# Four units of convolution in one stretch instead of two, on one Trainium2 core

## The chip, the core and the metric

The kernel runs on one core of one Trainium2 chip. A core has five engines with a queue of instructions each: TensorE (PE in the profile, with its weight loads shown apart as PEld), VectorE (DVE), ScalarE (ACT), GpSimd (POOL) and SyncE (SP), and 16 DMA engines that move data between HBM and the on-chip memory. PE writes into PSUM, a small memory of accumulators that DVE and ACT read. The metric is the time of one execution on the device in microseconds (us); lower is better. Engines run their own instructions in order and wait for each other by semaphores.

## What is computed

Two layers, one after the other, on x of shape 8 x 4160 x 192 (batch, sequence, channels). First a causal convolution over 7 positions, whose weights are a softmax and are shared by the 24 channels of each of 8 heads; then a channel mix, in which each position is blended with the one before it:

```python
x_pad = concat([zeros(B, 6, D), x], axis=1)
y     = einsum('hk,bskhg->bshg', softmax(weight), windows(x_pad, 7))   # B=8, S=4160, D=192
prev  = y shifted by one position
xk    = mu_k * y + (1 - mu_k) * prev
xr    = mu_r * y + (1 - mu_r) * prev
k     = relu(xk @ w_k)                    # 192 -> 1024
v     = (k * k) @ w_v                     # 1024 -> 192
out   = sigmoid(xr @ w_r) * v             # float32
```

## The kernel before

**Tiles.** Two batch rows form a pair, and four pairs are worked through one after the other. Channels come in thirds of 64 (`NC` = 3), so that 64 partitions hold one batch row of the pair and 64 the other. The sequence of a pair is cut in *steps* of 512 positions (a few of 256, and one short step at the end that collects the tails).

**Slots and bundles.** A step of 512 has eight *slots*; a slot is one tile of k: six matmuls (`k_mm`), a relu on ACT out of PSUM (`k_relu`), and a square on DVE (`k_square`). Four slots are a *bundle*, and the main loop runs over 65 bundles and a short end; two bundles make a step. Each bundle also has one *quad* of the last stage: `r` (12 matmuls) and its sigmoid `r_out` on ACT, `v_rows` in two halves of 32 matmuls, and `v_out`, a DVE product that reads v from PSUM and after which SP issues two writes to HBM. DVE also blends: `diff`, three `scale` and one `add_y` each for xk and xr, per step.

**Convolution.** It is done on PE as a product with a banded matrix (`toe`), in *units* `(g, c)`: a group `g` of four blocks of 120 positions (three in some groups), and a third `c`. `conv_t` issues eight matmuls a block, of up to 32 columns and 32 rows each, 32 matmuls for a unit of four blocks, and each matmul has its own weight load: 64 PE instructions a unit. `to_yT` then copies the unit from PSUM to `yT`, on ACT or on DVE. In the tables, units from group 3 on are dealt out two to a bundle, from bundle 1 to bundle 50, and `conv_pair` runs them. The first groups are done in the functions of the first bundles.

**The order of the work** is written out by hand (`bundle_rest` for bundle 3 and later). On PE a bundle is: two `k_mm`, a third, `r`, `v_rows` half 0, the fourth `k_mm`, the convolution's units in one stretch, `v_rows` half 1. Here the four `k_mm` are called k0 to k3, the halves v0 and v1. On DVE it is: the last square of the bundle before, a part of the blending, `v_out` of the quad before, more blending and three squares, and, in odd bundles, the copy of the second unit.

**PSUM.** One ring of four places of two banks serves all: each `k_mm`, `r`, `v` and each two units of convolution take one place, which comes free when what reads it is done. Where two engines read the same tile, the recorder lets the second wait for the first: a unit's copy on DVE waits for the copy on ACT of the other unit in that place.

**Loads.** x comes by DMAs that POOL issues (`load_x`, two or four for a group), into eight buffers (`xb`). They are put at the head of a bundle (table `early`), five bundles ahead of the group's first unit, and a tiny DVE memset in `x_tile` keeps them from starting before DVE has come so far. Groups 5 and 6 are loaded in bundle 1 (table `mix_a`), 7 in bundle 2.

**Instructions.** With every loop unrolled, PE's program has 19,957 instructions. A bundle with two units of four blocks has 328 of them: k0 to k2 36, `r` 24, v0 64, k3 12, convolution 128, v1 64. A bundle without convolution has 200.

Of the kernel before, what the change touches and what calls it, by code (L numbers as in the profile page):

```python
# [7 lines left out]
FP32 = mybir.dt.float32  # L8
# [6 lines left out]
def kernel(  # L15
# [11 lines left out]
    nc = tc.nc  # L27
# [5 lines left out]
    P = 128  # L33
# [5 lines left out]
    BANK = 512  # L39
# [13 lines left out]
    ring = ctx.enter_context(tc.tile_pool(name="ring", bufs=4, space=bass.MemoryType.PSUM))  # L53
# [21 lines left out]
    n = 0  # L75
# [9 lines left out]
    groups = []  # L85
# [66 lines left out]
    n = groups[0][2] * 2 * D  # L152
# [120 lines left out]
    def conv_t(g, c, o, blocks):  # L273

        for n, i in enumerate(blocks):
            for first_piece in (True, False):
                for s in range(2):
                    for q in range(2):
                        c0 = c * Q + q * 32
                        lo, hi = c0 // G, (c0 + 31) // G  # L280
                        h, m = (hi, 32) if first_piece else (lo, hi * G - c0)
                        p0 = s * Q + q * 32
                        nc.tensor.matmul(  # L283
                            out=o[p0 : p0 + m, n * BLK : (n + 1) * BLK],
                            lhsT=xbs[g][:, i, s, c0 : c0 + m],
                            rhs=toe[:, h, 0:BLK],
                            start=True,
                            stop=True,
                        )

    def to_yT(g, c, o, copy):
        p, base, nb = groups[g]
        n = min(nb * BLK, S - base)
        copy(out=yTs[p][:, c, YC + base : YC + base + n], in_=o[:, 0:n])  # L294

    def conv_pair(b):

        units = xt.get(b, [])
        if not units:
            return  # L300
        o = ring.tile([P, 2, BANK], FP32, tag="k", name="ps_t")
        for k, (g, c) in enumerate(units):
            if groups[g][1] == 0 and c == 0:
                new_yT(groups[g][0])
            conv_t(g, c, o[:, k, :], range(groups[g][2]))
        for k, (g, c) in enumerate(units):
            to_yT(g, c, o[:, k, :], nc.vector.tensor_copy if k and b % 2 else nc.scalar.copy)

    def new_yT(p):
        yTs[p] = two.tile([P, 3, -(-(YC + S) // 16) * 16], BF16, tag="yT", name="yT")  # L310
        nc.vector.memset(yTs[p][:, :, 0:YC], 0.0)
# [63 lines left out]
    def k_mm(n, cs=range(NC)):  # L375


        s, j = slots[n]
        L = steps[s][2]
        xk = xks[s]  # L380
        if cs[0] == 0 and n not in k_ps:
            k_ps[n] = ring.tile([P, 2, BANK], FP32, tag="k", name="ps_k")
        ps = k_ps[n]
        nf = STEP // L

        for c in cs:
            for f in range(nf):
                fs = slice((j * nf + f) * P, (j * nf + f + 1) * P)
                for i in range(2):
                    r = slice(i * Q, (i + 1) * Q)  # L390
                    nc.tensor.matmul(  # L391
                        out=ps[:, i, f * L : (f + 1) * L],
                        lhsT=wk[r, c, fs],
                        rhs=xk[r, c, :L],
                        start=c == 0 and f == 0,
                        stop=c == NC - 1 and f == nf - 1,
                    )

    def k_relu(n):
        ps = k_ps.pop(n)  # L400
        k_sb = four.tile([P, 2 * STEP], BF16, tag="k_sb", name="k_sb")
        k_sbs[n] = k_sb
        nc.scalar.activation(out=k_sb, in_=ps.rearrange("p a b -> p (a b)"), func=AF.Relu)  # L403

    def k_square(n):
        s, j = slots[n]
        L = steps[s][2]
        k_sb = k_sbs.pop(n)
        if j == 0:
            k2s[s] = three.tile([P, NF, 2 * STEP], BF16, tag="k2", name="k2")  # L410
        nf = STEP // L
        i = k_sb
        o = k2s[s][:, j, :]
        if nf > 1:
            i = k_sb.rearrange("p (b f t) -> p f b t", b=2, f=nf)
            o = k2s[s][:, j * nf : (j + 1) * nf, 0 : 2 * L].rearrange("p f (b t) -> p f b t", b=2)
        nc.vector.tensor_tensor(out=o, in0=i, in1=i, op=ALU.mult)  # L417
# [113 lines left out]
    early, rq, rs, xt, mix_a, mix_b, mix_c, vq, late = ({} for _ in range(9))  # L531

    def at(table, b, fn, *a):
        table.setdefault(b, []).append((fn, a))

    units = [(g, c) for g in range(3, len(groups)) for c in range(NC)]
    for n, u in enumerate(units):
        xt.setdefault(1 + n // 2, []).append(u)
    for g in range(5, len(groups)):
        b = max(1, 1 + (units.index((g, 0))) // 2 - 5)  # L540
        at(mix_a if b == 1 else early, b, x_tile, g)
        at(mix_a if b == 1 else early, b, load_x, g)
    for s, (p, t0, L, n0, ns) in enumerate(steps):
        fb = first_bundle[s]
        if s == 0:
# [26 lines left out]
    for s, j, vb in quads:  # L572
        b = vb - (s == LAST)
# [7 lines left out]
    def run(table, b, part=slice(None)):  # L581
        for fn, a in table.get(b, [])[part]:
            fn(*a)
# [86 lines left out]
    def bundle_second(b, ns):  # L670

        act_, dve_ = nc.scalar.copy, nc.vector.tensor_copy
        g = 2
        k_mm(ns[0])
        k_relu(ns[0])
        k_mm(ns[1])
        tiles = [ring.tile([P, 2, BANK], FP32, tag="k", name="ps_t") for _ in range(2)]
        outs = [tiles[0][:, 0, :], tiles[1][:, 0, :], tiles[0][:, 1, :]]
        conv_t(g, 0, outs[0], range(4))
        to_yT(g, 0, outs[0], dve_)  # L680
        k_relu(ns[1])
        conv_t(g, 1, outs[1], range(4))
        to_yT(g, 1, outs[1], dve_)
        k_mm(ns[2])
        k_relu(ns[2])
        conv_t(g, 2, outs[2], range(4))
        to_yT(g, 2, outs[2], act_)
        k_mm(ns[3])
        k_square(ns[0])
        run(mix_a, b)  # L690
        k_relu(ns[3])
        k_square(ns[1])
        run(mix_b, b)
        conv_pair(b)
        run(mix_c, b)
        run(late, b)

    def bundle_rest(b, ns):

        units = xt.get(b, [])  # L700
        quad = vq[b][0]
        if b == 3:
            for n in range(2):
                k_mm(ns[n])
                k_relu(ns[n])
            k_square(bundles[b - 1][2])
            k_square(bundles[b - 1][3])
            run(mix_a, b)
        else:
            if b == 4:  # L710
                v_out(*vq[b - 1][0])
            k_square(bundles[b - 1][3])
            run(mix_a, b)
            if b > 4:
                v_out(*vq[b - 1][0])
            for n in range(2):
                k_mm(ns[n])
                k_relu(ns[n])
        run(mix_b, b)
        k_square(ns[0])  # L720
        k_square(ns[1])
        run(mix_c, b)
        k_mm(ns[2])
        k_relu(ns[2])
        run(rq, b, slice(0, 1))
        if units:
            run(rs, b, slice(0, 1))
        v_rows(*quad, 0)
        if not units:
            run(rs, b, slice(0, 1))  # L730
        k_square(ns[2])
        k_mm(ns[3])
        k_relu(ns[3])
        run(rq, b, slice(1, None))
        run(rs, b, slice(1, None))
        conv_pair(b)
        v_rows(*quad, 1)
        run(late, b)

    def bundle_third(b, ns):  # L740

        quad = vq[b][0]
        for n in bundles[b - 1][2:]:
            k_square(n)
        run(mix_a, b)
        k_mm(ns[0])
        k_relu(ns[0])
        k_square(ns[0])
        k_mm(ns[1])
        k_relu(ns[1])  # L750
        run(rq, b)
        run(rs, b)
        v_rows(*quad, 0)
        conv_pair(b)
        k_square(ns[1])
        run(mix_b, b)
        run(mix_c, b)
        run(late, b)
        k_mm(ns[2])
        k_relu(ns[2])  # L760
        v_rows(*quad, 1, (0,))
        k_mm(ns[3])
        k_relu(ns[3])
        v_rows(*quad, 1, (1,))
        v_out(*quad)
# [56 lines left out]
```

## Time and profile before

| | |
|---|---|
| median of 3 runs | 449.6 us (448.69 to 449.67) |
| the profiled execution | 451.12 us, of which its span 449.4 us |
| PE busy | 436.4 us of the span |
| DVE, ACT, POOL busy | 388.4, 339.8, 71.5 us |
| granted PE clock | 0.999 of full speed |
| one bundle with two units, steady | 6.79 us (stretches of convolution start at 180.53, 187.31 and 194.10) |
| DMA traffic | 42.22 MB, 94 GB/s on average |

The profile is that of one execution. "Idle before" a group of instructions is time in which its engine had nothing running, with what ended the wait; "issue" there means that nothing which the profile shows held the engine back. PEld is the same engine as PE: weight loads run beside matmuls.

### The profile page before, as it was taken

The page shows a single profiled execution, that of the slowest core. Times are in us where ns is not written, and L with a number is a line of the kernel's source. Part 1 is how long each engine was busy: PE and PEld are TensorE (multiplying, and loading weights), DVE is VectorE, ACT ScalarE, POOL GpSimd, SP SyncE. Part 2 cuts the span into 40 slices and gives each one's busy share as a digit, 9 for nine tenths or more (in the row PEclk, how much of TensorE's full clock was granted, in tenths as well). Part 3 has the DMA queues.
Part 4 walks back from the last instruction along what each step waited for, and adds up shares of the span by engine and source line. Part 5 has one row for each costly group of instructions (what it writes and reads, how often), then busy time and mean ns, then how long its engine had stood idle before and what let it go on. Part 6 is the DMA issues. An engine that isn't in the chain of part 4 may idle for free.

```text
span 449.4 us, 21973 instructions
## 1 busy us (share of the span) xinstructions
PE 436.4 (97%) x9968; PEld 332.3 (74%) x9969; DVE 388.4 (86%) x712; ACT 339.8 (76%) x413; POOL 71.5 (16%) x111
## 2 busy tenths in 40 slices
PE   8689999999999999999999999999999999999996
PEld 5457777777777777777777777777777777777786
DVE  5879898988889888889888898888898899999983
ACT  6768778778678777787787787787787788887771
POOL 8422301111221202012211102122000000000000
PEclk9999999999999999999999999999999999999999
DMA  9995548454545546394555556383321122222223
GB/s 151 173 102 107 88 90 143 82 101 87 97 98 103 87 94 92 91 142 71 106 95 93 97 109 95 88 116 79 82 72 54 59 73 71 73 71 73 73 71 109
DMA packets 74782, 42.22 MB, mean 94 GB/s; under 512 B 39884, under 2 KB 74688, under 8 KB 74688
## 3 DMA queue, kind: packets, MB, share of 16 engines
q0 software_dynamic: 38448, 14.66, 29.9%
q1 hardware_dynamic: 35440, 25.59, 18.1%
q8 instruction: 78, 1.28, 1.2%
q10 hardware_dynamic: 800, 0.57, 0.4%
q14 instruction: 16, 0.13, 0.1%
HBM read 29.89 MB, written 25.56 MB: 123 GB/s over the span
## 4 chain that ended last, share of the span: by engine, by line
PE 94%; issue 2%; DMA 2%; POOL 1%; ACT 0%; DVE 0%; POOLq 0%; DVEq 0%
PE ps_v L479 38%; PE ps_k L391 37%; PE ps_t L283 11%; PE ps_r L448 7%; DMA wk<-in_moe_w_k_dram 2%; PE ps_v L431 1%; POOL wk L195 0%; POOL xb L123 0%; ACT k_sb L403 0%; DVE k L417 0%; ACT yT L294 0%; POOL tap L229 0%; DVE o_sb L515 0%; POOL band L257 0%; POOL band L254 0%
## 5 line engine op out<-in xcount | busy, mean ns | idle before, releaser
L403 ACT ACTIVATE k_sb<-ps_k 128x1024 bf16<-128x1024 f32 x260 | 252.3, 1024 | 86.9 <-PE ps_k L391 82.7
L391 PE MATMUL ps_k<-xk,wk 64*128 64x512 bf16 (+1 forms) x1632 | 191.3, 367 | 1.0 <-DMA wk<-in_moe_w_k_dram 0.7
L479 PE MATMUL ps_v<-wv,k 64*128 64x192 bf16 x4032 | 188.5, 243 | 0.7 <-DVE k L417 0.7
L417 DVE TENSOR_TENSOR k<-k_sb 128x1024 bf16<-128x1024 bf16 x260 | 173.8, 687 | 15.9 <-ACT k_sb L403 15.8
L479 PEld LDWEIGHTS <-k 64*128 64x128 bf16 x4032 | 166.2, 94 | 9.1 <-issue 0.9
L391 PEld LDWEIGHTS <-wk 64*128 64x128 bf16 x1632 | 80.7, 94 | 58.5 <-DMA wk<-in_moe_w_k_dram 1.1
L123 POOL DMA_DIRECT2D xb<-in_x_dram x70 | 52.4, 752 | 239.9 <-PE ps_v L479 83.9
L495 DVE TENSOR_TENSOR o_sb<-ps_v,r_sb 128x768 f32<-128x768 f32 x64 | 60.9, 952 | 8.4 <-PE ps_v L479 5.6
L283 PEld LDWEIGHTS <-xb 128*32 128x32 bf16 (+3 forms) x3360 | 45.7, 94 | 28.4 <-issue 27.6
L283 PE MATMUL ps_t<-toe,xb 128*32 128x120 bf16 (+3 forms) x3360 | 56.3, 219 | 5.5 <-issue 5.1
L459 ACT ACTIVATE r_sb<-ps_r 128x768 bf16<-128x768 f32 x65 | 53.6, 826 | 5.4 <-PE ps_v L479 4.7
L294 ACT CAST yT<-ps_t 128x480 bf16<-128x480 f32 (+3 forms) x81 | 41.5, 544 | 6.3 <-PE ps_t L283 5.8
L448 PEld LDWEIGHTS <-xr 64*128 64x128 bf16 x780 | 35.8, 94 | 13.3 <-issue 0.6
L448 PE MATMUL ps_r<-wr,xr 64*128 64x192 bf16 x780 | 43.0, 243 | 0.0
L294 DVE CAST yT<-ps_t 128x480 bf16<-128x480 f32 (+2 forms) x27 | 17.3, 643 | 26.3 <-ACT yT L294 25.3
L365 DVE TENSOR_SCALAR xr<-d,mu 128x512 bf16<-128x512 bf16 (+1 forms) x102 | 36.9, 366 | 0.0
L365 DVE TENSOR_SCALAR xk<-d,mu 128x512 bf16<-128x512 bf16 (+1 forms) x99 | 32.3, 358 | 0.1
L334 DVE TENSOR_TENSOR d<-yT 128x1536 bf16<-128x1536 bf16 (+4 forms) x36 | 31.1, 865 | 1.5 <-ACT yT L294 1.4
L371 DVE TENSOR_TENSOR xr<-xr,yT 128x1536 bf16<-128x1536 bf16 (+1 forms) x33 | 31.1, 942 | 1.1
L371 DVE TENSOR_TENSOR xk<-xk,yT 128x1536 bf16<-128x1536 bf16 (+3 forms) x33 | 30.3, 919 | 0.1
L318 POOL COPY y_tail<-yT 128x195 bf16<-128x195 bf16 x4 | 1.9, 477 | 44.0 <-ACT yT L294 43.9
L431 PE MATMUL ps_v<-wv,k 128*128 128x192 bf16 x64 | 5.5, 247 | 0.0
(50 smaller groups left out, 44.9 us busy)
## 6 DMA issues: line engine op xcount, KB each, us to landing
out_dram<-o_sb SPq DMA_DIRECT2D x128, 192.0 KB, 3.5
xb<-in_x_dram POOLq DMA_DIRECT2D x56, 192.0 KB, 4.6
xb<-in_x_dram POOLq DMA_DIRECT2D x8, 144.0 KB, 4.2
wk<-in_moe_w_k_dram POOLq DMA_DIRECT2D x4, 192.0 KB, 6.1
xb<-in_x_dram POOLq DMA_DIRECT2D x6, 96.0 KB, 3.2
wv<-in_moe_w_v_dram POOLq DMA_DIRECT2D x1, 384.0 KB, 8.5
xb<-in_x_dram POOLq DMA_DIRECT2D x6, 45.8 KB, 3.1
xb<-in_x_dram POOLq DMA_DIRECT2D x8, 32.2 KB, 3.7
```

The source lines that it names most:

```text
L123: nc.gpsimd.dma_start(out=xb[:, lo:hi, s, :], in_=bass.AP(tensor=x.tensor, offset=x.offset + (b * S + t0 + lo * BLK) * D, ap=[[D, P], [BLK ...
L283: nc.tensor.matmul(out=o[p0 : p0 + m, n * BLK : (n + 1) * BLK], lhsT=xbs[g][:, i, s, c0 : c0 + m], rhs=toe[:, h, 0:BLK], start=True, stop= ...
L294: copy(out=yTs[p][:, c, YC + base : YC + base + n], in_=o[:, 0:n])
L365: nc.vector.tensor_scalar(out=t[:, c, :L], in0=diffs[s][:, c, :L], scalar1=mu[:, i, c : c + 1], scalar2=None, op0=ALU.mult)
L371: nc.vector.tensor_tensor(out=o, in0=o, in1=y_of(s, sl, 0), op=ALU.add)
L391: nc.tensor.matmul(out=ps[:, i, f * L : (f + 1) * L], lhsT=wk[r, c, fs], rhs=xk[r, c, :L], start=c == 0 and f == 0, stop=c == NC - 1 and f ...
L403: nc.scalar.activation(out=k_sb, in_=ps.rearrange("p a b -> p (a b)"), func=AF.Relu)
L417: nc.vector.tensor_tensor(out=o, in0=i, in1=i, op=ALU.mult)
L448: nc.tensor.matmul(out=ps[:, i, k * D : (k + 1) * D], lhsT=xr[q, c, ts], rhs=wr[q, c, :], start=c == 0, stop=c == NC - 1,)
L459: nc.scalar.activation(out=r_sbs[s, j], in_=r_ps.pop((s, j))[:, :, 0 : 2 * D], func=AF.Sigmoid)
L479: nc.tensor.matmul(out=v_ps[s, j][:, bank, k * D : (k + 1) * D], lhsT=k2s[s][q, f, t * P : (t + 1) * P], rhs=wv[q, f, :], start=half == 0 ...
L495: nc.vector.tensor_tensor(out=o_sb.rearrange("p (b t) d -> p b (t d)", b=2), in0=v_ps.pop((s, j)), in1=r_sbs.pop((s, j)), op=ALU.mult,)
```

## The change

Units from the eleventh on are dealt out four at a time, to bundles 6, 8, 10 and so on up to 48 (bundle 50 keeps the single unit that is left, and the odd bundles from 7 on have none). `conv_units` takes one place of the ring for each two units, runs all units of the bundle in one stretch on PE, and then copies them; in a bundle of four, units 0 and 2 are copied by ACT, 1 and 3 by DVE; in a bundle of two, both by ACT. The loads of x are put five bundles ahead of the bundle that now has the group's first unit, but not before bundle 2, always at its head: groups 5 and 6 move from bundle 1 to bundle 2.

```diff
-    def conv_pair(b):
+    def conv_units(b):
 
         units = xt.get(b, [])
-        if not units:
-            return
-        o = ring.tile([P, 2, BANK], FP32, tag="k", name="ps_t")
+        outs = []
         for k, (g, c) in enumerate(units):
             if groups[g][1] == 0 and c == 0:
                 new_yT(groups[g][0])
-            conv_t(g, c, o[:, k, :], range(groups[g][2]))
+            if k % 2 == 0:
+                tile_ = ring.tile([P, 2, BANK], FP32, tag="k", name="ps_t")
+            outs.append(tile_[:, k % 2, :])
+            conv_t(g, c, outs[k], range(groups[g][2]))
         for k, (g, c) in enumerate(units):
-            to_yT(g, c, o[:, k, :], nc.vector.tensor_copy if k and b % 2 else nc.scalar.copy)
+            to_yT(g, c, outs[k], nc.vector.tensor_copy if k % 2 and len(units) > 2 else nc.scalar.copy)
...
     for n, u in enumerate(units):
-        xt.setdefault(1 + n // 2, []).append(u)
+        xt.setdefault(1 + n // 2 if n < 10 else 6 + (n - 10) // 4 * 2, []).append(u)
     for g in range(5, len(groups)):
-        b = max(1, 1 + (units.index((g, 0))) // 2 - 5)
-        at(mix_a if b == 1 else early, b, x_tile, g)
-        at(mix_a if b == 1 else early, b, load_x, g)
+        b = max(2, min(k for k in xt if (g, 0) in xt[k]) - 5)
+        at(early, b, x_tile, g)
+        at(early, b, load_x, g)
```

In the three functions that write out a bundle, the call of `conv_pair(b)` becomes `conv_units(b)`, in the same place.

More of the change, by code (lines that the diff above doesn't have):

```diff
@@ L693, in bundle_second @@
         run(mix_b, b)
-        conv_pair(b)
+        conv_units(b)
         run(mix_c, b)
@@ L735, in bundle_rest @@
         run(rs, b, slice(1, None))
-        conv_pair(b)
+        conv_units(b)
         v_rows(*quad, 1)
@@ L753, in bundle_third @@
         v_rows(*quad, 0)
-        conv_pair(b)
+        conv_units(b)
         k_square(ns[1])
```

## The prediction, made before the changed kernel ran

> **What bounds the kernel now.** I read the shares of the page, then the chain of waits, then PE's timeline at three places, since the change acts on PE's queue.
>
> ```profile
> PE 436.4 (97%) x9968; PEld 332.3 (74%) x9969; DVE 388.4 (86%) x712; ACT 339.8 (76%) x413; POOL 71.5 (16%) x111
> q8 instruction: 78, 1.28, 1.2%
> PE 94%; issue 2%; DMA 2%; POOL 1%; ACT 0%; DVE 0%; POOLq 0%; DVEq 0%
> ```
>
> PE is busy for 97% of the span, and 94% of the chain that ended last is PE; DVE at 86% and ACT at 76% release in time. So the time falls only by what leaves PE's queue or its gaps, and rises by any new gap. The q8 line matters below: 78 packets in 1.28 MB are 16.4 KB each, and 19,957 PE instructions over 78 are 256, so PE's program arrives in pages of 256 instructions.
>
> The price of a stretch is read at the end of the convolution, where it thins out (start, length of the group, engine, line):
>
> ```profile
> 344.34 1.49 PE L479 MATMUL ps_v<-wv,k 64*128 64x192 bf16 x32
> ...
> 350.17 0.81 PE L283 MATMUL ps_t<-toe,xb 128*32 128x120 bf16 x48
> 350.92 1.50 PE L479 MATMUL ps_v<-wv,k 64*128 64x192 bf16 x32
> ...
> 356.75 0.50 PE L283 MATMUL ps_t<-toe,xb 128*32 128x120 bf16 x24
> 357.18 1.50 PE L479 MATMUL ps_v<-wv,k 64*128 64x192 bf16 x32
> ...
> 362.91 1.48 PE L479 MATMUL ps_v<-wv,k 64*128 64x192 bf16 x32
> ```
>
> From one v1 to the next is 6.58 us with 48 matmuls of convolution, 6.26 with 24, 5.73 with none; with 64 a bundle takes 6.79. From 24 to 64 that is 0.53 us for 40 matmuls, 13.25 ns each (6.6 ns per instruction). Drawn back to none it leaves 6.79 - 64 x 0.01325 - 5.73 = 0.21 us that a stretch costs whatever its length.
>
> The gaps are read at the start:
>
> ```profile
> 17.10 0.75 PE L283 MATMUL ps_t<-toe,xb 128*16 128x120 bf16 x43 [0.98 <-issue]
> 17.78 0.82 PE L391 MATMUL ps_k<-xk,wk 64*128 64x512 bf16 x6
> 18.53 0.60 PE L283 MATMUL ps_t<-toe,xb 128*32 128x120 bf16 x32
> 19.07 0.82 PE L391 MATMUL ps_k<-xk,wk 64*128 64x512 bf16 x6
> 19.82 0.75 PE L283 MATMUL ps_t<-toe,xb 128*32 128x120 bf16 x41
> 23.30 0.49 PE L283 MATMUL ps_t<-toe,xb 128*32 128x120 bf16 x23 [2.73 <-issue]
> 23.73 1.47 PE L391 MATMUL ps_k<-xk,wk 64*128 64x512 bf16 x12
> 25.03 0.66 PE L448 MATMUL ps_r<-wr,xr 64*128 64x192 bf16 x12
> 25.53 1.48 PE L479 MATMUL ps_v<-wv,k 64*128 64x192 bf16 x32
> 26.94 0.81 PE L283 MATMUL ps_t<-toe,xb 128*32 128x120 bf16 x48
> 29.15 0.40 PE L283 MATMUL ps_t<-toe,xb 128*32 128x120 bf16 x16 [1.39 <-issue]
> ```
>
> Three gaps lie inside convolutions, where no data is new. Between the first and the second are 43+6+32+6+41 = 128 matmuls, with their weight loads 256 instructions; between the second and the third 23+12+12+32+48 = 127, one page again. PE waits for its next page. In short windows of the DMA view the instruction packets stand at 14.55, 20.90 and 26.85 us, and PE resumes at 17.10, 23.30 and 29.15: 2.3 to 2.5 us after each (I take 2.4). A packet is asked for when the page before it begins (one page ahead) and may queue among the x loads: 3.5 us from 23.30 to 26.85. Counting page starts through the program (193 + 256n) finds 49 in bundles 3 to 50. Packets follow them by 0.1 to 2.7 us, and no page there lasts under 4.1 us, so they nearly always come in time (missed at 119.5 by 0.26 us and at 161.7 by 0.94).
>
> **Part 1, fewer stretches.** Bundles 1 to 50 have 50 stretches now and 28 after. 22 x 0.21 = **-4.6 us**, all on PE, the bound. The matmuls are the same ones.
>
> **Part 2, longer stretches eat pages faster.** Four full units are exactly 256 instructions and last 256 x 6.6 ns + 0.2 = 1.9 us; a page that falls together with them lasts 1.9 us instead of at least 4.1. What is behind PE there is everything. The nearest row is the three gaps: 2.4 us from packet to resumption. The delay before the packet, for pages that begin in the first 50 instructions of a stretch, was 0.40, -0.03, 0.65, 0.55, 0.07, 0.01, 0.71 us in quiet cases (mean 0.34; negative since the queue is read ahead of execution) and 1.35 to 1.81 in four where DMAs were moving data. So a page needs 2.74 us quietly, 3.9 loaded. Quiet is the case I take: output writes move data from 0.8 to 2.4 us after `v_out` ends (184.75 to 186.4 after 183.98), which puts the odd bundle's writes just ahead of the stretch, and x loads now start behind a stretch, some 9 us before the next.
>
> The changed program's page starts, counted the same way, lie in the 22 stretches at instructions 39, 151, 5, 117, 229, 37, 149, 5, 117, 19, 131, 243, 99, 211, 67, 194, 81, 193, 49, 161, 17 and 129. A page that starts at o lasts (256 - o) x 6.6 ns + 0.1 for the stretch's end + o x 20.8 ns of v1 (1.33 us for 64): 1.86 us at o = 5, 2.03 and 2.06 at 17 and 19, 2.33 at 37 and 39, 2.49 at 49. Against 2.74 that is missing: 2 x 0.88 + 0.71 + 0.68 + 0.41 + 0.41 + 0.25 = 4.2. Pages that end late in a stretch were asked for in v0, with a median delay of 0.2, so need 2.6: 243 lasts 2.47 (0.1 short), 229 lasts 2.66, 211 2.9, all else over 3. Sum **+4.3 us**. Bounds: with no delay before the packet (2.4) it is +2.1; with 3.1, +8.4; with 3.5, +14.
>
> [...] The gaps one page apart, with the packet 0.1 to 0.6 us after the crossing when quiet, are the row of a one-page lookahead, and I go by the row.
>
> **Part 3, x of groups 5 and 6.** Their four DMAs issue at 19.62 to 22.58 and keep the packet of 26.85 waiting, which makes the third gap, 1.39 us. In bundle 2 the memsets stand behind the `diff` that ends at 25.9; the packet asked for at 23.30 then meets a quiet queue and serves the crossing at 27.76. The first two gaps are from loads issued before 15 us and stay. The next page is asked for at 27.8 among six loads (groups 5 to 7): with the same 3.5 us + 2.4 it is there at 33.7, its crossing at 35.2 (36.60 less 1.39). Group 5, first used in bundle 4 near 42 us, lands by 33. **-1.3 us**; bounds -1.4 and 0, if DVE, busy from 27 to 31 us, ends the bundle instead.
>
> **Part 4, the copies.** DVE loses its copy in bundles 1 to 49 with two units and gets two in each bundle of four: 46 instead of 27 in all, 19 x 0.65 = 12.4 us more, ACT as many fewer. The row is an odd bundle of before:
>
> ```profile
> 188.98 0.66 DVE L294 CAST yT<-ps_t 128x480 bf16<-128x480 f32 x1 [0.91 <-ACT yT L294]
> 190.43 0.95 DVE L495 TENSOR_TENSOR o_sb<-ps_v,r_sb 128x768 f32<-128x768 f32 x1
> ```
>
> With T the start of a stretch (187.31), DVE copies at T+1.67, after ACT's copy. In a bundle of four: relu of k3 to T+1.15, ACT's copy 0 to 1.64, DVE's copy 1 from 1.67 to 2.33, ACT's copy 2 after the second place is written (T+1.8 + 0.12) to 2.48, DVE's copy 3 from 2.50 to 3.16. Queued behind it: the square, a `scale`, `v_out`, which started 1.45 us after the copy and now does at T+3.95, ending at 4.9. Who waits: `r` of the next bundle takes v's place, at T + 1.9 + 1.33 + 1.95 = 5.15. k1 and k2 take the places of the units, at T+3.9 and 4.6, long free. So it is hidden, with 0.2 us to spare; it costs what `v_out` is later than that. DVE's idle time catches up in the odd bundle, which has no copy and 5.73 us, as the bundles after 357 us run. The second place in a stretch was `r`'s, whose sigmoid ended at 187.22, before T. **0 us**, bounds 0 and +4 (0.2 in each of 22).
>
> **Part 5, other late pages.** The 1.2 us lost at 119.5 and 161.7 go, as all pages shift, and others meet the same loads: 0, bounds -1.2 and +2.
>
> Sum: -4.6 + 4.3 - 1.3 = **-1.6 us**: the profiled execution from 451.1 to 449.5, its span to 447.8; it lies 1.5 above the median, so the median goes from 449.6 to **448.0**.
>
> **Rivals.**
> [...]
> - *Pages come later still*, the other side: the place is v1 behind a stretch, the price per page its delay; it decides from 2.87 us a page (sum +5.9). At 3.1 the sum is +8.4 - 5.9 = +2.5, 452.1 us; at 3.5, 458. For it the four loaded cases out of eleven. 0.25.
> - *DVE becomes the bound*: `v_out` is late by 0.2 or more in each bundle of four, +4: 452. DVE is at 86%; against it the slack above. 0.07.
> - *The early gap only moves*: 449.3. 0.05.
> - My forecast, page sums from 2.1 to 5.5: 445.8 to 449.2, 0.50.
>
> **How the numbers follow.** A measurement of this kernel tells about 0.2%, 0.9 us, from no change. Faster than 448.7: 0.40 of mine + 0.13 hidden = 0.53. Within: 0.10 of mine, 0.05 of later pages, 0.05 moved gap, 0.02 of DVE = 0.22. Slower: 0.20 + 0.05 = 0.25. The range takes in mine, half of the hidden pages' case, DVE's, and later pages up to 3.1: 445.0 to 452.1.
>
> **What would show it.** Gaps "issue" of 0.4 to 0.9 us on PE in v1 or late in a stretch, in about seven of the 22, at the counted places, the largest at the two with o = 5; bundles of four some 7.6 us and odd ones 5.73; no third gap near 28 us. Wrong if v1 behind o = 5 starts without a gap, if gaps stand before `r` with DVE named, or if most of the 22 have one.

## The result, and the profile after

| | before | after |
|---|---|---|
| median of 19 runs each | 449.67 us (448.38 to 451.35) | 447.43 us (445.37 to 449.11) |
| ratio of the times | | 0.995 (95%: 0.9934 to 0.9966) |
| profiled execution, its span | 451.12, 449.4 us | 449.11, 447.4 us |
| granted PE clock in it | 0.999 | 0.995 |
| a bundle of four and the one behind it, undisturbed | 13.57 us (two bundles of two) | 13.36 us |

The time fell by 2.2 us, 0.5%. PE is still the bound. The shares, the chain of waits and the costliest group of copies in the page of the changed kernel:

```profile
PE 433.9 (97%) x9969; PEld 337.5 (75%) x9969; DVE 398.3 (89%) x731; ACT 333.5 (75%) x394; POOL 71.9 (16%) x111
PE 91%; DVE 2%; DMA 2%; issue 2%; POOL 1%; ACT 0%; DVEq 0%; POOLq 0%; ACTq 0%
L294 DVE CAST yT<-ps_t 128x480 bf16<-128x480 f32 (+2 forms) x46 | 29.3, 641 | 14.0 <-ACT yT L294 13.1
```

DVE has 46 copies, as counted, and its share rose from 86% to 89%, but only 2% of the chain is DVE's (0% before). PE's busy time fell by 2.5 us.

PE's timeline of the changed kernel at bundles 10, 24 and 46 (start, length of the group, engine, line; in brackets the idle time before it):

```profile
82.92 1.86 PE L283 MATMUL ps_t<-toe,xb 128*32 128x120 bf16 x128
84.72 0.26 PE L480 MATMUL ps_v<-wv,k 64*128 64x192 bf16 x2
85.62 1.41 PE L480 MATMUL ps_v<-wv,k 64*128 64x192 bf16 x30 [0.65 <-issue]
...
177.56 1.86 PE L283 MATMUL ps_t<-toe,xb 128*32 128x120 bf16 x128
179.36 0.58 PE L480 MATMUL ps_v<-wv,k 64*128 64x192 bf16 x9
180.42 1.15 PE L480 MATMUL ps_v<-wv,k 64*128 64x192 bf16 x23 [0.47 <-issue]
...
327.53 1.86 PE L283 MATMUL ps_t<-toe,xb 128*32 128x120 bf16 x128
329.32 0.50 PE L480 MATMUL ps_v<-wv,k 64*128 64x192 bf16 x8
330.36 1.17 PE L480 MATMUL ps_v<-wv,k 64*128 64x192 bf16 x24 [0.54 <-issue]
```

The long stretches run whole, and v1 behind them stops after 2, 9 and 8 matmuls. With their weight loads these are 4, 18 and 16 instructions, and the counted page ends stand 5, 19 and 17 instructions into v1: PE stops where its page ends, and no engine is named. This is the mechanism that part 2 counts.

Where the 2.0 us between the two spans lie: from the start to the stretch of bundle 3, 1.16 us (36.60 to 35.44); from there to bundle 50, 0.84 (320.15 to 319.31); behind it nothing (92.65 in both). The first part is not shown to come from the change: the second gap already ends 1.25 us earlier (at 22.05 for 23.30), and PE's instructions are the same up to there.

In the middle the sum closes. 22 stretches fewer at 0.21 are -4.6. The changed kernel's steps, from one stretch of four to the next, last 5.85 us more than undisturbed ones (13.36 with 128 matmuls, 13.25 ns less for each matmul fewer). The kernel before lost 2.1 there: three late pages, at 114.98, 119.53 and 162.68 (0.53, 0.29, 0.95), and two waits of `r` for `v_out`, at 232.43 and 313.68 (0.20 and 0.16). All five are gone. -4.6 + 5.85 - 2.1 = -0.85.

By bundle of four, in us; "offset" is the instruction of the stretch at which a page begins, "lost" is the whole step's loss, and the two rows under it are what of it is lost where a page begins and where `r` waits for `v_out`. The ten bundles not shown were predicted at 0 and lost 0.02 at most:

| bundle | 6 | 10 | 14 | 16 | 20 | 24 | 28 | 32 | 36 | 40 | 42 | 46 |
|---|---|---|---|---|---|---|---|---|---|---|---|---|
| offset | 39 | 5 | 229 | 37 | 5 | 19 | 243 | 211 | 194 | 193 | 49 | 17 |
| predicted | .41 | .88 | 0 | .41 | .88 | .68 | .1 | 0 | 0 | 0 | .25 | .71 |
| lost | .41 | .83 | .39 | .15 | .07 | .71 | .91 | .31 | .13 | .26 | .97 | .71 |
| at a page | .41 | .83 | 0 | 0 | .07 | .71 | .44 | .31 | .13 | .26 | .97 | .71 |
| at `r` | 0 | 0 | .35 | .15 | 0 | 0 | .47 | 0 | 0 | 0 | 0 | 0 |

So pages cost 4.8 us, in ten bundles, and waits of `r` 1.0. (The 0.04 left over in bundle 14 is about what its step, which has 24 matmuls more than the others, takes longer in kernels without a wait there.) One wait of `r` is long enough for the timeline to name what ended it, in the step of bundle 28; the DVE product comes first, then `r`:

```profile
215.72 0.94 DVE L496 TENSOR_TENSOR o_sb<-ps_v,r_sb 128x768 f32<-128x768 f32 x1
216.71 0.67 PE L449 MATMUL ps_r<-wr,xr 64*128 64x192 bf16 x12 [0.31 <-DVE o_sb L496]
```

The others leave PE idle for less than the 0.15 us from which the timeline prints it. Here are the larger two, in the steps of bundles 14 and 16:

```profile
120.63 0.95 DVE L496 TENSOR_TENSOR o_sb<-ps_v,r_sb 128x768 f32<-128x768 f32 x1
121.64 0.67 PE L449 MATMUL ps_r<-wr,xr 64*128 64x192 bf16 x12
...
128.42 0.94 DVE L496 TENSOR_TENSOR o_sb<-ps_v,r_sb 128x768 f32<-128x768 f32 x1
129.41 0.67 PE L449 MATMUL ps_r<-wr,xr 64*128 64x192 bf16 x12
```

In all three `r` starts 0.05 us after `v_out` ends, and 0.68, 0.49 and 0.35 us after the start of the last matmul of k, where 0.21 is usual. A fourth, at 115.61, costs 0.07. In the second bundle behind a stretch `v_out` has nothing to spare: in 21 of 22 `r` starts 0.05 us after its end, mostly without a loss above 0.02.

At the start the third gap is gone, but something else has come. PE's timeline of the changed kernel, to be held against the start shown in the prediction:

```profile
18.95 0.75 PE L283 MATMUL ps_t<-toe,xb 128*32 128x120 bf16 x41
22.05 0.50 PE L283 MATMUL ps_t<-toe,xb 128*32 128x120 bf16 x23 [2.34 <-issue]
22.48 2.23 PE L392 MATMUL ps_k<-xk,wk 64*128 64x512 bf16 x12
24.50 1.17 PE L449 MATMUL ps_r<-wr,xr 64*128 64x192 bf16 x12
25.45 1.97 PE L480 MATMUL ps_v<-wv,k 64*128 64x192 bf16 x32
27.36 1.02 PE L283 MATMUL ps_t<-toe,xb 128*32 128x120 bf16 x64
```

The stretch at 27.36 runs whole, where before it was cut by 1.39 us. But 12 matmuls of k took 2.23 us against 1.47 before, `r` 1.17 against 0.66, v0 1.97 against 1.48. The table of stretches of the same execution (from:to, then busy us of PE, with its instructions, PEld, DVE, ACT, POOL, then the granted PE clock, the DMA share and GB/s; the number ahead of PE is the length) says why:

```profile
22.00:23.00 1.00, 0.95 (x29) 0.62 (x31) 1.00 (x3) 0.41 (x1) 1.00 (x2) 1.00 0.05 6
23.00:24.00 1.00, 1.00 (x8) 0.33 (x6) 0.16 (x1) 1.00 (x3) 1.00 (x2) 0.52 0.57 31
24.00:25.00 1.00, 1.00 (x12) 0.64 (x10) 0.43 (x1) 0.79 (x2) 1.00 (x3) 0.50 1.21 145
25.00:26.00 1.00, 1.00 (x18) 0.97 (x14) 0.46 (x2) 1.00 (x2) 1.00 (x2) 0.50 1.60 190
26.00:27.00 1.00, 1.00 (x22) 0.98 (x20) 1.00 (x3) 0.52 (x1) 0.85 (x2) 0.77 1.19 111
```

For about 3.4 us the granted clock was half (0.50). The profiled execution of before has 1.00 in all of these windows. So between these two executions the third gap's gain is paid back: from the end of the second gap to bundle 3 it took 13.39 us after and 13.30 before. The fall is not peculiar to the changed kernel. The mean clock of a run tells the two sorts apart: in nine of the 19 runs of the changed kernel it is 0.994 to 0.996, and their mean time is 448.2 us; in the ten at 0.998 to 1.0 it is 446.8. Of the 57 runs of the kernel before that were made beside the experiments, 29 have a mean clock of 0.991 to 0.996. The profiled execution of before is one without the fall, that of after one with it, and the longest of its 19.

### The profile page after: what moved, and what is told of

Its sections match the earlier page's. It is cut to its first block, busy times and chain, and to the rows that moved or that the text cites. A ratio compares the mean times of both kernels' runs of the same rounds, so it can differ in the third digit from the quotient of the medians.

```text
span 447.4 us, 21974 instructions
## 1 busy us (share of the span) xinstructions
PE 433.9 (97%) x9969; PEld 337.5 (75%) x9969; DVE 398.3 (89%) x731; ACT 333.5 (75%) x394; POOL 71.9 (16%) x111
## 4 chain that ended last, share of the span: by engine, by line
PE 91%; DVE 2%; DMA 2%; issue 2%; POOL 1%; ACT 0%; DVEq 0%; POOLq 0%; ACTq 0%
PE ps_v L480 37%; PE ps_k L392 35%; PE ps_t L283 10%; PE ps_r L449 7%; DMA xb<-in_x_dram 2%; PE ps_v L432 1%; DVE o_sb L496 1%; POOL wk L195 1%; POOL xb L123 1%; DVE k L418 1%; DVE xr L366 0%; ACT k_sb L404 0%; DVE xk L372 0%; DVE xk L366 0%; ACT r_sb L460 0%
## 5 line engine op out<-in xcount | busy, mean ns | idle before, releaser
L480 PEld LDWEIGHTS <-k 64*128 64x128 bf16 x4032 | 169.3, 94 | 14.1 <-issue 3.5
L392 PEld LDWEIGHTS <-wk 64*128 64x128 bf16 x1632 | 84.0, 94 | 55.8 <-DMA wk<-in_moe_w_k_dram 1.4
L283 PE MATMUL ps_t<-toe,xb 128*32 128x120 bf16 (+3 forms) x3360 | 51.8, 217 | 3.9 <-issue 3.4
L294 ACT CAST yT<-ps_t 128x480 bf16<-128x480 f32 (+3 forms) x62 | 33.1, 543 | 12.4 <-PE ps_t L283 12.2
L294 DVE CAST yT<-ps_t 128x480 bf16<-128x480 f32 (+2 forms) x46 | 29.3, 641 | 14.0 <-ACT yT L294 13.1
L366 DVE TENSOR_SCALAR xr<-d,mu 128x512 bf16<-128x512 bf16 (+1 forms) x102 | 35.3, 350 | 0.0
L366 DVE TENSOR_SCALAR xk<-d,mu 128x512 bf16<-128x512 bf16 (+1 forms) x99 | 34.3, 376 | 0.1
```

The costliest lines, as they stand in the source:

```text
L283: nc.tensor.matmul(out=o[p0 : p0 + m, n * BLK : (n + 1) * BLK], lhsT=xbs[g][:, i, s, c0 : c0 + m], rhs=toe[:, h, 0:BLK], start=True, stop= ...
L366: nc.vector.tensor_scalar(out=t[:, c, :L], in0=diffs[s][:, c, :L], scalar1=mu[:, i, c : c + 1], scalar2=None, op0=ALU.mult)
L392: nc.tensor.matmul(out=ps[:, i, f * L : (f + 1) * L], lhsT=wk[r, c, fs], rhs=xk[r, c, :L], start=c == 0 and f == 0, stop=c == NC - 1 and f ...
L480: nc.tensor.matmul(out=v_ps[s, j][:, bank, k * D : (k + 1) * D], lhsT=k2s[s][q, f, t * P : (t + 1) * P], rhs=wv[q, f, :], start=half == 0 ...
```

## The experiments

All ten kernels compute the whole result. The first four below were timed beside each other, then the next four, then the last two; ratios are to the kernel before of the same group.

**Is it the page, or the place in the program?** 64 more PE instructions ahead of the loop move all page starts 64 instructions to the front in every stretch; the work in the loop stays the same.

```diff
-    SHORT = 78
+    SHORT = 110
```

> The changed kernel with 32 more one-column warm-up matmuls at the start (110 instead of 78), which are 64 PE instructions, so every later page of 256 instructions begins 64 instructions earlier in the work. Nothing else differs. Theory (a stretch stalls when a page that lasts under about 2.7 us runs out): the gaps move with the page starts. Of the 22 stretches of four, gaps are expected in bundles 12, 16, 22, 30, 34, 38, 42 and perhaps 6, the largest (0.6 to 0.9 us) in 34 and 38, and none in 10, 20, 24 and 46, where the changed kernel has its largest but one. Sum of the gaps in the stretches some 2.3 to 3.5 us. Rival (gaps belong to a place in the kernel: DMA traffic, a wait for a copy or for PSUM): gaps stay in bundles 6, 10, 14, 24, 42 and 46.

Measured: 447.37 us, 0.9925 (0.9899 to 0.9951). Two bundles in PE's timeline of this kernel, 38 and 46:

```profile
272.67 1.86 PE L283 MATMUL ps_t<-toe,xb 128*32 128x120 bf16 x128
274.46 0.50 PE L480 MATMUL ps_v<-wv,k 64*128 64x192 bf16 x8
275.65 1.17 PE L480 MATMUL ps_v<-wv,k 64*128 64x192 bf16 x24 [0.68 <-issue]
...
327.62 1.86 PE L283 MATMUL ps_t<-toe,xb 128*32 128x120 bf16 x128
329.41 1.49 PE L480 MATMUL ps_v<-wv,k 64*128 64x192 bf16 x32
```

Bundle 38, which lost nothing in the changed kernel, now has its page end 17 instructions into v1 and the gap behind eight matmuls; bundle 46 had that and now runs through. Seven of the eight bundles that the count names lose time (6, 12, 16, 30, 34, 38, 42). The eighth, 22, doesn't: with groups of three blocks its stretch has 104 matmuls, not 128, and the page that begins in it lasts 4.21 us. The count doesn't name five others that lose 0.14 to 0.53 us at a page (10, 20, 24, 26, 28); but for 26, their pages begin 179 to 211 instructions into the stretch. Bundle 14 loses its 0.39 as in the changed kernel, at `r` and not at a page. So the gaps go with the pages, and the pages that end late in a stretch are dearer than the prediction took them.

The ratio itself says less. The second gap at the start is shorter here (1.47 us for 2.34), and none of the six runs has the low mean clock. At 0.998 to 1.0 the changed kernel's mean was 446.8 us, and this one's is 447.3.

**Only the stretches that should lose, only those that should gain.** The first kernel keeps four units in the ten bundles for which the count gave a gap or the traces of the changed kernel showed one, the second in the other twelve (36 and 40, with the smallest losses, among them); elsewhere units go two to a bundle.

```diff
-        xt.setdefault(1 + n // 2 if n < 10 else 6 + (n - 10) // 4 * 2, []).append(u)
+        b4 = 6 + (n - 10) // 4 * 2
+        xt.setdefault(b4 if n >= 10 and b4 in (6, 10, 14, 16, 20, 24, 28, 32, 42, 46) else 1 + n // 2, []).append(u)
```

> Four units in one stretch only in ten bundles, 6, 10, 14, 16, 20, 24, 28, 32, 42 and 46, whose pages begin or end badly (the profile of the changed kernel has its gaps there); two units to a bundle elsewhere; loads at bundle 2 as in the changed kernel. PE's instructions before each of these stretches are as many as in the changed kernel, so the pages lie the same. Theory: loads -1.3, ten stretches fewer -2.1, page gaps +4.0 to +5 us: +0.6 to +1.6 us against the kernel before, ratio 1.001 to 1.004. Rival (each stretch of four is worth the same, whatever its page): loads -1.3 and 10/22 of the rest of the gain, some -1.7 us, ratio 0.996.

Measured: 449.71 us, 0.9985 (0.9963 to 1.0007). The ten steps lose .02, .48, .40, .16, .15, .78, 0, .19, .76 and .72 us, 3.66 together (of the .40, in bundle 14, .28 is `r` waiting), against 10 x 0.21 saved. By that alone it should be 1.5 us slower; it isn't, since no other step loses anything, and the 2.1 us that the kernel before loses elsewhere are gone here too. The expectation left that out; the interval holds neither its 1.001 nor the rival's 0.996.

```diff
...
+        xt.setdefault(b4 if n >= 10 and b4 in (8, 12, 18, 22, 26, 30, 34, 36, 38, 40, 44, 48) else 1 + n // 2, []).append(u)
```

> The counterpart: four units in one stretch only in the other twelve of the 22 bundles, two units to a bundle elsewhere. Theory: loads -1.3, twelve stretches fewer -2.5, page gaps at most +0.4: -3.4 us, ratio 0.992, below the changed kernel by some 1 us, and no gap of over 0.3 us at a stretch of four. Rival (each stretch worth the same): -1.8 us, ratio 0.996, above the changed kernel.

Measured: 445.33 us, 0.9883 (0.9858 to 0.9909), and no step of four loses more than 0.32 us. It beats the changed kernel. Two steps with two units to a bundle lose 0.41 and 0.97 us at late pages; all its steps together lose 1.9. Between bundles 3 and 50 the two traces differ by 2.2 us, as they should by two more saved stretches and the losses: 0.4 + 3.66 - 1.9. The medians differ by 4.4; in the traces the other 2.2 lie ahead of bundle 3 (35.02 and 32.86 us), where the clock fell in the first (mean clock of the execution 0.994) and not in the second (1.000).

**Shorter stretches, more often.** Three units in two of every three bundles, 96 matmuls to a stretch.

```diff
-        xt.setdefault(1 + n // 2 if n < 10 else 6 + (n - 10) // 4 * 2, []).append(u)
+        m = n - 10
+        xt.setdefault(1 + n // 2 if n < 10 else 6 + m // 6 * 3 + m % 6 // 3, []).append(u)
```

> From bundle 6 on three units in one stretch in two bundles of three, none in the third, so 35 stretches instead of 50 before and 28 in the changed kernel; a page that begins with such a stretch lasts 192 x 6.6 ns + 0.1 + 64 x 20.8 ns = 2.7 us at the least. Theory: loads -1.3, 15 stretches fewer -3.2, no page gaps but those of DMA traffic: -4.5 us, ratio 0.990, faster than the changed kernel by some 2 us. Rival (what counts is the number of stretches, and gaps are from elsewhere): 15/22 of the changed kernel's gain on stretches, some -2 us, ratio 0.9955.

Measured: 449.37 us, 0.9982 (0.9959 to 1.0005): a miss. Three bundles undisturbed take 20.15 us, against 20.35 before, so the stretches save what they should. The gaps eat it (1.37, 1.14 and 0.99 us are the largest). PE's timeline of the largest, at 84.33 us, and then the windows of the same execution (columns as above):

```profile
81.33 1.44 PE L283 MATMUL ps_t<-toe,xb 128*32 128x120 bf16 x96
82.70 0.26 PE L480 MATMUL ps_v<-wv,k 64*128 64x192 bf16 x2
84.33 1.41 PE L480 MATMUL ps_v<-wv,k 64*128 64x192 bf16 x30 [1.37 <-issue]
```

```profile
79.50:80.00 0.50, 0.50 (x18) 0.50 (x14) 0.35 (x1) 0.50 (x2) 0.00 (x0) 1.00 1.58 188
82.00:82.50 0.50, 0.50 (x55) 0.50 (x46) 0.08 (x1) 0.50 (x2) 0.00 (x0) 1.00 1.05 325
83.00:83.50 0.50, 0.00 (x0) 0.00 (x0) 0.50 (x1) 0.42 (x1) 0.00 (x0) 1.00 0.07 9
```

The page that ends the gap was asked for at 79.6 us, when x loads were moving 188 GB/s. Its packet stands at 82.0, 2.4 us later, and PE resumes 2.3 us after the packet, as it does at the start of the program. In this kernel the rule "five bundles ahead" puts the loads of every second group, from the eleventh on, at the head of a bundle that has a stretch; in the changed kernel it puts them all, from bundle 3 on, into odd bundles, of which those from 7 on have none.

**The same three units, loads in quiet bundles.** PE's program is that of the last kernel; only the bundles at whose heads x loads stand are others, from group 11 on always one without convolution.

```diff
...
-        b = max(2, min(k for k in xt if (g, 0) in xt[k]) - 5)
+        b = max(2, min(k for k in xt if (g, 0) in xt[k]) - 4)
+        b = max(2, b - (b - 8) % 3) if b > 2 else b
```

> The kernel with three units a stretch in two bundles of three, but every load of x from group 9 on put at the head of a bundle that has no convolution (four to six bundles ahead). In the run without this, long gaps of 0.99 to 1.37 us followed pages whose packet came 2.2 to 2.4 us after it was asked for, while x loads moved data. Theory (a packet queues behind x loads): delays fall under 1 us for the pages asked for ahead of a stretch, the gaps of about 1 us go, and the time falls by some 3 us on that kernel, to a ratio near 0.990. Rival (the long gaps of that run were not from x loads): as before, 0.998.

Measured: 444.96 us, 0.9887 (0.985 to 0.9923). PE's timeline at the same place:

```profile
82.77 1.44 PE L283 MATMUL ps_t<-toe,xb 128*32 128x120 bf16 x96
84.14 1.53 PE L480 MATMUL ps_v<-wv,k 64*128 64x192 bf16 x32
85.50 2.12 PE L392 MATMUL ps_k<-xk,wk 64*128 64x512 bf16 x18
```

No gap of 0.2 us is left behind bundle 3. Moving loads alone is worth 4.4 us here by the medians, and 4.6 by the traces from bundle 3 to the last stretch (313.85 and 309.29 us).

**The changed kernel with its loads one bundle later**, so that they stand at the heads of the bundles of four.

```diff
-        b = max(2, min(k for k in xt if (g, 0) in xt[k]) - 5)
+        b = max(2, min(k for k in xt if (g, 0) in xt[k]) - 4)
```

> The changed kernel with its x loads four bundles ahead instead of five, so that from group 8 on they stand at the head of the bundles that have a stretch of four, and move data from about 2 us after that to the stretch. Nothing else differs. Theory: packets for pages asked for ahead of and in a stretch come 1 to 2.5 us later than in the changed kernel, so pages that were just in time miss too: gaps in 12 or more of the 22, of 1 to 2 us each, +6 to +15 us on the changed kernel, ratio 1.01 to 1.03. Rival (the gaps have nothing to do with x loads; the data come in time either way): no change against the changed kernel, 0.995.

Measured: 465.87 us, 1.035 (1.0313 to 1.0386), 18 us more than the changed kernel, with the same PE instructions; more than expected. Its trace is of its longest execution (473.57 us), so its gaps are read for their place and not for their size. PE's timeline at bundle 24:

```profile
186.26 1.86 PE L283 MATMUL ps_t<-toe,xb 128*32 128x120 bf16 x128
188.06 0.58 PE L480 MATMUL ps_v<-wv,k 64*128 64x192 bf16 x9
192.04 2.08 PE L480 MATMUL ps_v<-wv,k 64*128 64x192 bf16 x23 [3.40 <-issue]
```

It is the gap of the changed kernel, behind the same nine matmuls, with 3.40 us in place of 0.47. The packet stands at 189.88 us, 3.5 after the page before begins (0.12 in the changed kernel), and PE resumes 2.2 us later. Pages are late in 13 of the 22 bundles. Not all of the 18 us is pages: the mean granted clock of this trace is 0.977, that of the changed kernel's 0.995 (of the five other runs, four have 0.987 or 0.988), and the 23 matmuls of v1 behind the gap shown took 2.08 us, where the changed kernel's 23 took 1.15.

**The loads alone, and the units alone.** The kernel before with groups 5 and 6 loaded in bundle 2, and the changed kernel with them back in bundle 1.

```diff
-        b = max(1, 1 + (units.index((g, 0))) // 2 - 5)
-        at(mix_a if b == 1 else early, b, x_tile, g)
-        at(mix_a if b == 1 else early, b, load_x, g)
+        b = max(2, 1 + (units.index((g, 0))) // 2 - 5)
+        at(early, b, x_tile, g)
+        at(early, b, load_x, g)
```

> The kernel before, with only the loads of groups 5 and 6 moved from bundle 1 to the head of bundle 2; the convolution stays at two units a bundle. Theory: the third gap (1.39 us near 28 us) goes, the rest stays: -1.3 us, ratio 0.997. Rival (DVE ends bundle 2 anyway, or the gap moves): 1.000.

Measured: 449.14 us, 0.9986 (0.9966 to 1.0006). PE's timeline of this kernel shows the stretch that was cut by 1.39 us in one piece:

```profile
23.70 1.48 PE L479 MATMUL ps_v<-wv,k 64*128 64x192 bf16 x32
25.11 1.02 PE L283 MATMUL ps_t<-toe,xb 128*32 128x120 bf16 x64
26.07 0.82 PE L391 MATMUL ps_k<-xk,wk 64*128 64x512 bf16 x6
```

```diff
-        b = max(2, min(k for k in xt if (g, 0) in xt[k]) - 5)
-        at(early, b, x_tile, g)
-        at(early, b, load_x, g)
+        b = max(1, min(k for k in xt if (g, 0) in xt[k]) - 5)
+        at(mix_a if b == 1 else early, b, x_tile, g)
+        at(mix_a if b == 1 else early, b, load_x, g)
```

> The changed kernel with the loads of groups 5 and 6 back in bundle 1. Theory: the gap near 28 us is back, +1.3 us on the changed kernel: ratio to the kernel before 0.998. Rival: as the changed kernel, 0.995.

Measured: 448.3 us, 0.9963 (0.9941 to 0.9985). Its third gap is only 0.21 us: the clock fell in the profiled execution (0.50 from 22 to 25 us), PE was slower (12 matmuls of k took 2.74 us for 1.47), and the page had more time (from the end of the second gap PE had work for 6.09 us, to 27.87, where the kernel before had 4.46). The loads are worth 449.79 - 449.14 = 0.65 us by the first kernel, and 0.9963 - 0.995, 0.6 us, by the second; neither interval excludes 0, nor the 1.3 that was expected. The second figure can't be told from the clock: 11 of that kernel's 12 runs have the low mean clock, against nine of 19 of the changed kernel, which at 1.4 us between the two sorts is worth 0.6 by itself. What the traces do show is the packet: behind the second gap it comes 3.59 and 4.06 us after the page before begins in the two traces with these loads in bundle 1, and 1.24 to 2.92 us in the ten others.

**All copies on ACT.**

```diff
-            to_yT(g, c, outs[k], nc.vector.tensor_copy if k % 2 and len(units) > 2 else nc.scalar.copy)
+            to_yT(g, c, outs[k], nc.scalar.copy)
```

> The changed kernel with all copies of the convolution from bundle 6 on done by ACT, so DVE has 44 copies (some 28 us of busy time) less and nothing of the stretch stands ahead of v_out on DVE. Theory (DVE's part is hidden): as the changed kernel, ratio 0.994 to 0.996; the one wait of PE for v_out (0.31 us near 216.7 us) goes. Rival (DVE late at each stretch costs time): 2 to 4 us faster than the changed kernel, ratio under 0.991. A third way, that ACT with four copies in a row holds up the relu of the next bundle: slower than the changed kernel, 0.998 or more.

Measured: 447.83 us, 0.9934 (0.9912 to 0.9956), which can't be told from the changed kernel. The four waits of `r` for `v_out` that cost time are gone, and the page gaps are in the same bundles, and in 14 and 16 as well. So those waits, 1.0 us, come with DVE's copies, and the gaps in stretches and v1 don't. In this trace the pages took 0.9 us more than in the changed kernel's, which hides the gain; which of the two copies is the better is not shown.

**The good stretches and quiet loads.** The kernel of the twelve, with any x load that would stand at the head of a bundle of four put one bundle ahead.

```diff
...
+        b -= b > 2 and len(xt.get(b, ())) > 2
```

> The kernel with four units in a stretch only in the twelve bundles whose pages lie well, with the x loads that stood at the head of one of these bundles put one bundle earlier. The run without this had 0.4 to 1.0 us lost in a few steps behind x loads. Theory: these mostly go, some -1 us, ratio 0.986; against the kernel with three units and quiet loads (0.9887) no clear difference. Rival: no change, 0.988.

Measured: 445.52 us, 0.9889 (0.9863 to 0.9915): a miss, no better than without it (0.9883). The edit could do little: it moves only the loads of groups 14 and 31, from bundles 12 and 38, and in the trace without it neither step loses anything. All but one of the steps of this trace lose less than 0.15 us. The three best kernels (twelve stretches of four, the same with quiet loads, three units with quiet loads) stand within 0.6 us of each other, 1.1% below the kernel before.

## Why the prediction was right, step by step

The time lay at 447.4 where 448.0 was predicted. The mechanism was the one told; four of its terms were off, in both directions, and that the sum came so near is in part luck.

- **Part 1** (-4.6) held: 13.57 to 13.36 us for an undisturbed pair of bundles is 0.21 a stretch.
- **Part 2** (+4.3) was 4.8 in the profiled execution. The term for pages that begin in the first 50 instructions came out at 3.7 (predicted 4.2), though not each: one of the two at offset 5 lost 0.07 where 0.88 was expected, one at 37 nothing at its page, and the one at 49 lost 0.97. From where the page before begins to where PE resumes, the gaps behind bundles 6, 10, 24 and 46 measure 2.70, 2.67, 2.73 and 2.72 us (bundle 10: 82.92 + 5 x 0.0066 to 85.62), so the need of 2.74 was well taken; its split was less so, since the packets stand 0.2 us before to 0.3 after the page begins and PE resumes 2.4 to 2.9 after them, where 0.34 and 2.4 were taken. In bundle 42 it is 3.44 us, with the packet 0.8 late; in bundles 16 and 20, whose packets came 0.1 and 0.3 us early, less than the need. The condition "wrong if v1 behind o = 5 starts without a gap" was met, but for the 0.07, in one of its two bundles. The mis-sized term was "Pages that end late in a stretch", 0.1 us in all: four of the five cost 0.44, 0.31, 0.13 and 0.26, 1.1 us. Their packets came 0.32, 0.76, 0.90 and 0.90 us after the page before begins, where 0.2 was taken. Those pages are asked for in v0 just ahead; that they meet the quad's output writes there fits, but no run took the writes away. (Of the sums, the bound for no delay is 1.9 by the lengths given, not 2.1, and the page starts in bundles 3 to 50 are 61, not 49; neither changes the forecast.)
- The chances give 0.13 to hidden pages, a case in which part 2 costs nothing and parts 1 and 3 alone make -5.9, 443.7 us. No run shows that term. What the runs show in its place is gaps that stand at the page ends, end 2.2 to 2.9 us after a packet and move by 64 instructions when 64 are put in front. With packets that stand 0.2 us before to 0.3 after the page before begins (bundles 6, 10, 24 and 46), that fits a lookahead of one page.
- That part 2 could be had at **"quiet"** prices rests on the x loads standing behind a stretch and not ahead of one. This decided the sign: with the loads one bundle later the same program takes 18 us more.
- **Part 3** (-1.3): the third gap went, as predicted, from the profiles of the changed kernel and of the loads alone. The runs give it about 0.6 us, not clear of 0. The profile of before had 1.39; one execution with the loads in bundle 1 in which the clock fell had 0.21, and the low mean clock comes in about half of the runs of the kernel before (29 of 57).
- **Part 4** (0) was +1.0 in the trace. The 0.2 us to spare was worked out for the first bundle behind a stretch, where two of the four waits stand (0.07 and 0.14). The other two (0.28 and 0.47) are in the second, where "DVE's idle time catches up" was to hold and `v_out` has nothing to spare. The sign "if gaps stand before `r` with DVE named" came true, in one bundle by the timeline.
- **Part 5** (0) was wrong, -2.1. Of the late pages of before it had read two, 1.2 us; there are three, 1.75, and two waits of `r`, 0.36. "Others meet the same loads" was the failed step: the loads of the changed kernel start, from group 8 on, only in odd bundles, where a page lasts long enough for the next to come late. In its trace the latest packet behind bundle 3, at 296.8 us, comes some 2.9 us after the page before begins, and PE, which needs it near 300.1, runs on without a gap of 0.15 us there.

Together, -4.6 + 4.8 - 0.6 + 1.0 - 2.1 = -1.5, as the -1.6 predicted, because part 5 hid the errors of the parts 2, 3 and 4 (0.5, 0.7 and 1.0). Measured were -2.2, with an interval of the ratio that reaches from -3.0 to -1.5; the 0.7 between is not placed.

Hidden pages fall by the gaps. Of the rivals, pages later still was the right worry, held off by where the loads stand. DVE as the bound falls by the kernel with all copies on ACT, which is not faster beyond the noise.

Still open: what sets each single packet's delay, and why `r` waits for `v_out` in these four bundles and hardly in the others.

## What to carry to other kernels

The stretch of 256 short instructions was here a demand on the instruction queue too: a page that began 5 instructions into it was 1.84 us of work (bundle 10, 2.67 us less the 0.83 lost), and from where such a page began to where PE went on with the next, 2.7 us passed (2.67 to 2.73 in bundles 6, 10, 24 and 46). So count a stretch's instructions in pages (256 here), and compare the two times. If they are close, put bulk loads elsewhere than just ahead of the dense stretch (that was worth 4.4 us with three units, and the other way cost 18 with four), and choose the stretches whose page ends fall well (2.2 us between bundles 3 and 50, the twelve against the ten). When one part of a change moves transfers, ask what stalls of the old order go as well as what new ones come.

## What was not expected of the hardware

- A page that meets x loads can be very late: 2.4 us from the crossing to the packet, and a gap of 1.37 us in v1 in one kernel; 3.5 us to the packet and a gap of 3.40 in another.
- A gap on PE was followed in some executions by half of the granted clock: in the changed kernel's, a gap of 2.34 us by 0.50 for about 3.4 us (23.0 to about 26.4), which made 12 matmuls of k take 2.23 us for 1.47; with the loads back in bundle 1, a gap of 2.48 us by 0.50 from 22 to 25 us. In others, with a gap as long or longer, it was followed by none: 2.73 us in the kernel before, 2.58 with the loads alone. Why it depends on the execution, no run here tests.
